# GpSimd steps that wait for the VectorE step ahead of them in a written plan

## The chip, the cores and the metric

The kernel runs on one core of a Trainium2 chip. Times are device microseconds of that core. The core has TensorE (PE: matrix products; PEld is its loading of weights), VectorE (DVE), ScalarE (ACT), GpSimd (POOL) and SyncE (SP), which here issues the transfers (DMA). Each engine works off its own instructions in order, and a semaphore makes one engine wait for another.

## What is computed

A chain of three layers on 3072 tokens with 256 channels (8 heads of 32). First an attention-like scan with decay, then two dense layers with nonlinearities (ELU, then Mish). Cut to what matters:

```python
def _attn_ref(x, a, B, C):                    # x 4x8x768x32, B and C 4x8x768x16
    log_a = np.log(np.clip(a, 1e-06, 1.0))
    state = np.zeros((batch, H, N, D))
    for c in range(S // 32):                  # chunks of 32 in the reference
        cum = np.cumsum(la, axis=-1)
        L = np.exp(cum[:, :, :, None] - cum[:, :, None, :]) * causal
        M = np.einsum('bhin,bhjn->bhij', Cc, Bc) * L
        y[:, :, sl] = (np.einsum('bhij,bhjd->bhid', M, xc)
                       + np.einsum('bhin,bhnd->bhid', Cc, state) * np.exp(cum)[..., None])
        Bx = np.einsum('bhjn,bhjd->bhjnd', Bc, xc) * np.exp(cum[:, :, -1:] - cum)[..., None, None]
        state = np.exp(np.sum(la, axis=-1))[..., None, None] * state + np.sum(Bx, axis=2)

h = x @ w_in;   g = np.where(h > 0, h, np.exp(np.minimum(h, 0)) - 1);          x = g @ w_out    # 256 -> 2048 -> 256
h = x @ w_in2;  g = h * np.tanh(np.log1p(np.exp(h)));                          y = g @ w_out2
```

## The kernel before

**Tiling.** The scan works on 32 tiles of 96 tokens of one batch (`T = 96`; 8 chunks by 4 batches). The dense layers work on seven blocks of tokens (`BL`: two of 384, four of 512, one of 256) in slots: 16 slots of 128 hidden channels for a layer and block. In a slot TensorE makes `h` (L780 to L782, written `emit_h`), the nonlinearity makes `w` from it, `w` is split into a high part `gh` (L366 or L368) and a low part `gl` (L823), and TensorE adds its product with the output weights to `acc` (L848 in the first block, L843 to L845 in layer 1, L874 and L875 in layer 2). The products that matter are made of three parts, high by high, low by high, high by low, so weights too are split: `raw` is put in order by L340 or L342, L351 and L358, its high part is taken by a cast (`job_4`: L366 on ScalarE, L368 on VectorE), its low part by a subtraction (`job_5`, L382 on GpSimd or VectorE). ELU is `elu_1` to `elu_3` (L796, L802 or L804, L810 or L812), Mish is L827. When a block of layer 1 is through, `acc` becomes the input of layer 2 by L855 (high, `xyh`) and L859 (low, `xyl`).

**The scan's steps.** For a tile a row of cumulated decays is loaded to all partitions (`d<-cum_d`), L553 subtracts (GpSimd or VectorE), L557 masks (GpSimd), L562 takes the exponential (ScalarE); `B` and `C` are split into three bf16 parts (L523, L528, L534, L540), transposed by DMA (L544), and TensorE makes scores (L670, or L658 in the first tiles), which L676 (L664) multiplies with the decays. GpSimd also makes `bw` (L567, L576) and the scaled `C` (L586), which L608 transposes on VectorE. L707 and L737 are the products of the tile with `x` and the new chunk state, L719 and L724 its split output.

**What sets the order.** No scheduler reorders this program. All work is written as steps: `step(opts, *deps, dl=...)` holds for each engine that could do it a cost, a function that emits its instructions, the steps it needs and a due time. `run_steps` plays the steps through once at build time, engine by engine, each time taking the most urgent one that can begin, and writes down for each step a begin time and the engine chosen. It keeps a list `lock` of the VectorE steps that can hold the SBUF port that VectorE and GpSimd share: the weight steps L342, L358, L368 and L382, the splits L528 and L540, L553, the copy behind L608, L804, and the splits `gh` and `gl`. In the plan a GpSimd step does not overlap one of these: `held[V]` and `held[G]` keep the end of the last on either side. At the end the steps are sorted by planned begin, and their functions are called in this order:

```python
        place = {k: i for i, (_, k, _) in enumerate(order)}
        for _, _, k, o in sorted((t, place[k], k, o) for t, k, o in order):
            steps[k][0][o][2]()
```

That fixes the order on each engine. Semaphore waits are put in by the layer below, for data and buffers alone. On the chip nothing holds GpSimd to the plan's order against VectorE: a GpSimd instruction starts when its data, its buffer and its own queue allow it.

Of the kernel before, what the change touches and what calls it, by code (L numbers as in the profile page):

```python
# [18 lines left out]
def tile_chain(  # L19
# [12 lines left out]
    nc = tc.nc  # L32
# [24 lines left out]
    at = ctx.enter_context(tc.tile_pool(name="at", bufs=1))  # L57
# [10 lines left out]
    steps = []  # L68
    A, V, G, PE, DQ = "act", "dve", "pool", "pe", "sp"
# [9 lines left out]
    lock = set()  # L79
# [3 lines left out]
    def step(opts, *deps, dl=1e9):  # L83
        steps.append((opts if isinstance(opts, list) else [opts], deps, dl))
        return len(steps) - 1
# [37 lines left out]
    def run_steps():  # L123
# [37 lines left out]
        while todo:  # L161
            k = todo.pop()
# [23 lines left out]
        def urgency(k, e):  # L186
            return late[k] + (HOLD if loads(k, e) else 0.0)
# [4 lines left out]
        def opened(k):  # L192
            for o, (e, cost, *_) in enumerate(steps[k][0]):
                open_[e].append((k, o, ready(k, e), cost))
# [11 lines left out]
        order = []  # L206
        for _ in range(n):
# [24 lines left out]
            t, e, can = best  # L232
            k, o, r, cost = min((c for c in can if c[2] <= t + 0.02), key=lambda c: (urgency(c[0], e), c[0]))
# [17 lines left out]
            for q in succ[k]:  # L251
                left[q] -= 1
                if not left[q]:
                    opened(q)
        place = {k: i for i, (_, k, _) in enumerate(order)}
        for _, _, k, o in sorted((t, place[k], k, o) for t, k, o in order):
            steps[k][0][o][2]()


    c_t, b_t, c96_t, x_t = {}, {}, {}, {}  # L260
# [496 lines left out]
    order = [(1, 0), (1, 1), (2, 0), (2, 1), (1, 2)]  # L757
# [37 lines left out]
    def elu_1(s):  # L795
        nc.scalar.activation(out=new_w(s), in_=st[s][0], func=AF.Exp)  # L796

    def elu_2(s, eng):
        w = st[s][1]
        st[s].append(eng)  # L800
        if eng == A:
            nc.scalar.activation(out=w, in_=w, func=AF.Relu, scale=-1.0, bias=1.0)  # L802
        else:
            nc.vector.tensor_scalar(out=w, in0=w, scalar1=1.0, scalar2=1.0, op0=ALU.min, op1=ALU.subtract)  # L804

    def elu_3(s):
        h, w, eng = st[s]
        st[s].pop()
        if eng == A:
            nc.vector.scalar_tensor_tensor(out=w, in0=w, scalar=-1.0, in1=h, op0=ALU.mult, op1=ALU.max)  # L810
        else:
            nc.vector.tensor_tensor(out=w, in0=h, in1=w, op=ALU.max)  # L812
# [13 lines left out]
    def mish_1(s):  # L826
        nc.scalar.activation(out=new_w(s), in_=st[s][0], func=AF.Mish)  # L827
# [49 lines left out]
    def y2_out1(c, k, eng):  # L877
        n = min(128, BL[c] - 128 * k)
        o = tl["o", c, k] = at.tile([128, DM], F32, tag="o", name="o", bufs=2)[0:n]
        if eng == V:  # L880
            nc.vector.tensor_scalar_mul(o, acc[2, c, k][:, 1], 1.0 / WS)
        else:
            nc.scalar.activation(out=o, in_=acc[2, c, k][:, 1], func=AF.Copy, scale=1.0 / WS)

    def y2_out2(c, k):
        o = tl["o", c, k]
        nc.vector.scalar_tensor_tensor(
            out=o, in0=acc[2, c, k][:, 0], scalar=1.0 / WS, in1=o, op0=ALU.mult, op1=ALU.add
        )
# [18 lines left out]
    def alt(f, *opts):  # L908

        return [(e, cost, lambda e=e: f(e)) for e, cost in opts]  # L910
# [256 lines left out]
    for s in range(len(order) * NF):  # L1167
# [23 lines left out]
        if layer == 1:  # L1191
            e = step((A, ca, lambda s=s: elu_1(s)), h, wn)
            table[e] = "exp"
            e = step(alt(lambda e, s=s: elu_2(s, e), (V, cv), (A, ca + 0.04)), e)
            lock.add(e)
            e = step((V, ct, lambda s=s: elu_3(s)), e)
        else:
            e = step((A, ca, lambda s=s: mish_1(s)), h, wn)
# [30 lines left out]
        else:  # L1229
            prev = YS.get(s - 1, [])  # L1230
            YS[s] = []
            for k in range(NK[c]):
# [4 lines left out]
                if f == NF - 1:  # L1237
                    of, on = take("o")
                    o = step(alt(lambda e, c=c, k=k: y2_out1(c, k, e), (A, 0.27), (V, 0.33)), y, on)
                    o = step((V, 0.35, lambda c=c, k=k: y2_out2(c, k)), o)  # L1240
                    q = step((DQ, 1.0, lambda c=c, k=k: y2_store(c, k), 0.36), o)
                    of.append(q)
                    acc_f[blk][k][0].append(o)
    run_steps()


# [28 lines left out]
```

## Time and profile before

| | |
|---|---|
| Runs | 622.65, 623.7, 625.8 us; median 623.7 |
| Profiled execution | 624.2 us, its span from the first to the last instruction 622.5 us |
| Busy, share of the span | PE 97%, PEld 82%, DVE 72%, ACT 61%, POOL 31% |
| Mean granted TensorE clock | 0.985 of 2.4 GHz |
| DMA | 47.09 MB, 46.29 MB of them on SyncE's queue |

The share of PE is an average over stages: in some it never pauses, in others it waits. How to read the rows further down: a row of the windows is a stretch of the execution with the busy time of each engine in it and its instructions in brackets; a row of the timeline is one instruction or a few alike, with start, duration, engine, line, what it writes from what, and in square brackets how long the engine was idle before it and what ended that.

### The profile page before, as it was taken

To read this page: it belongs to the slowest core of one execution; us is meant where nothing else is said; L and a number is where in the kernel's file an instruction comes from. 1 tells how busy PE (TensorE), PEld (TensorE's weight loads), DVE (VectorE), ACT (ScalarE), POOL (GpSimd) and SP (SyncE) were. 2 spreads that over 40 slices of the span, in tenths; PEclk is the share of its full clock that TensorE was granted. 3 is DMA by queue.
4 is the path that set the end of the run, shared out by engine and by line. 5 is a ranking of instruction groups with operands and counts; after the bars stand their busy time and mean duration, and the time that the engine had idled before them with its cause. 6 is when DMAs were issued, how large, how long until landed. Compare 5 with 4: busy or idle time off the path is not lost.

```text
span 622.5 us, 10990 instructions
## 1 busy us (share of the span) xinstructions
PE 602.3 (97%) x3876; PEld 508.4 (82%) x3876; DVE 450.5 (72%) x948; ACT 377.3 (61%) x705; POOL 191.6 (31%) x238
## 2 busy tenths in 40 slices
PE   6899989999999999999999999989999999999997
PEld 5777779989887878888887888877888888988896
DVE  4899988997798898765778865778865445744444
ACT  3699879976878865544687644588544214652121
POOL 2366455323554564201644501346200000200000
PEclk9599989999999999999999999999999999999999
DMA  7599893302647553001454301534200000100010
GB/s 159 162 261 292 261 246 86 60 12 55 128 85 89 112 98 85 11 0 28 84 110 75 87 1 14 107 63 99 56 4 1 0 1 4 34 1 0 1 35 17
DMA packets 133655, 47.09 MB, mean 76 GB/s; under 512 B 116672, under 2 KB 122432, under 8 KB 133600
## 3 DMA queue, kind: packets, MB, share of 16 engines
q1 hardware_dynamic: 133488, 46.29, 33.9%
q8 instruction: 30, 0.49, 0.3%
q14 instruction: 25, 0.20, 0.1%
q10 hardware_dynamic: 112, 0.10, 0.0%
HBM read 32.31 MB, written 3.24 MB: 57 GB/s over the span
## 4 chain that ended last, share of the span: by engine, by line
PE 77%; DVE 6%; ACT 6%; DMA 4%; issue 3%; SPq 2%; POOL 1%; DVEq 0%; POOLq 0%; ACTq 0%
PE acc L874 13%; PE h L780 12%; PE h L781 12%; PE h L782 12%; PE acc L875 6%; PE acc L843 6%; PE acc L844 6%; PE acc L845 6%; PE ys L707 2%; DMA t<-stk 1%; DMA bc<-in_B_dram 1%; PE s L670 1%; DMA xs<-in_x_dram 1%; DVE gl L823 1%; DVE raw L358 1%
## 5 line engine op out<-in xcount | busy, mean ns | idle before, releaser
L780 PE MATMUL h<-xyh,wi 128*128 128x512 f32 (+2 forms) x448 | 168.6, 376 | 2.0 <-ACT w L827 1.6
L781 PE MATMUL h<-xyl,wi 128*128 128x512 f32 (+2 forms) x448 | 162.0, 362 | 0.3 <-DVE xyl L724 0.3
L782 PE MATMUL h<-xyh,wi 128*128 128x512 f32 (+2 forms) x448 | 161.7, 361 | 0.0
L874 PE MATMUL acc<-wo,gh 128*128 128x512 f32 x384 | 142.6, 403 | 0.0
L823 DVE TENSOR_TENSOR gl<-w,gh 128x512 fp32r<-128x512 f32 (+2 forms) x181 | 119.2, 660 | 20.9 <-ACT gh L366 13.0
L827 ACT ACTIVATE w<-h 128x512 f32<-128x512 f32 (+2 forms) x112 | 59.4, 536 | 103.0 <-PE h L782 67.8
L875 PE MATMUL acc<-wo,gl 128*128 128x256 f32 x384 | 107.7, 280 | 0.2 <-DVE gl L823 0.2
L368 DVE CAST gh<-w 128x512 fp32r<-128x512 f32 (+2 forms) x114 | 47.8, 420 | 74.6 <-PE acc L874 50.3
L780 PEld LDWEIGHTS h<-xyh,wi 128*128 128x128 f32 x448 | 84.8, 189 | 19.0 <-ACT w L827 3.6
L782 PEld LDWEIGHTS h<-xyh,wi 128*128 128x128 f32 x448 | 84.9, 189 | 10.6
L781 PEld LDWEIGHTS h<-xyl,wi 128*128 128x128 f32 x448 | 85.0, 190 | 9.8 <-DVE xyl L724 0.7
L874 PEld LDWEIGHTS acc<-wo,gh 128*128 128x128 f32 x384 | 72.2, 188 | 15.4
L796 ACT ACTIVATE w<-h 128x512 f32<-128x512 f32 (+2 forms) x96 | 51.7, 539 | 54.6 <-PE h L782 34.7
L823 POOL TENSOR_TENSOR gl<-w,gh 128x512 fp32r<-128x512 f32 (+2 forms) x27 | 31.2, 1156 | 173.3 <-ACT gh L366 112.2
L875 PEld LDWEIGHTS acc<-wo,gl 128*128 128x128 f32 x384 | 72.6, 189 | 2.7 <-DVE gl L823 0.5
L843 PE MATMUL acc<-gh,wo 128*128 128x512 f32 (+2 forms) x192 | 71.0, 370 | 3.0 <-DVE xyl L859 3.0
L366 ACT ACTIVATE gh<-w 128x512 fp32r<-128x512 f32 (+2 forms) x94 | 54.8, 583 | 28.8 <-PE acc L844 22.5
L845 PE MATMUL acc<-gl,wo 128*128 128x512 f32 (+2 forms) x192 | 70.2, 366 | 0.0
L844 PE MATMUL acc<-gh,wo 128*128 128x512 f32 (+2 forms) x192 | 70.2, 365 | 0.0
L804 DVE TENSOR_SCALAR w<-w 128x512 f32<-128x512 f32 (+2 forms) x74 | 32.9, 444 | 26.0 <-ACT w L796 25.0
L812 DVE TENSOR_TENSOR w<-h,w 128x512 f32<-128x512 f32 (+2 forms) x74 | 46.6, 631 | 1.5
L843 PEld LDWEIGHTS acc<-gh,wo 128*128 128x128 f32 x192 | 36.7, 191 | 8.4 <-DVE xyl L859 3.4
(102 smaller groups left out, 847.8 us busy)
## 6 DMA issues: line engine op xcount, KB each, us to landing
d<-cum_d SPq DMA_DIRECT2D x31, 288.0 KB, 3.8
raw<-in_moe_w_in_dram SPq DMA_DIRECT2D x16, 512.0 KB, 6.7
raw<-in_moe_w_out_dram SPq DMA_DIRECT2D x16, 512.0 KB, 5.9
xs<-in_x_dram SPq DMA_DIRECT2D x32, 96.0 KB, 2.9
bc<-in_C_dram SPq DMA_DIRECT2D x32, 48.0 KB, 2.6
bc<-in_B_dram SPq DMA_DIRECT2D x32, 48.0 KB, 2.6
out_dram<-o SPq DMA_DIRECT2D x15, 96.0 KB, 1.9
bc<-bc SPq DMA_DIRECT2D x84, 16.0 KB, 2.4
```

The source lines that it names most:

```text
L366: nc.scalar.activation(out=out, in_=in_, func=AF.Copy)
L780: nc.tensor.matmul(out=h, lhsT=hi[:, k, fs], rhs=xh[:, k, :], start=(k == 0), stop=False)
L781: nc.tensor.matmul(out=h, lhsT=hi[:, k, fs], rhs=xl[:, k, :], start=False, stop=False)
L782: nc.tensor.matmul(out=h, lhsT=lo[:, k, fs], rhs=xh[:, k, :], start=False, stop=(k == 1))
L796: nc.scalar.activation(out=new_w(s), in_=st[s][0], func=AF.Exp)
L823: alu(eng).tensor_tensor(out=gl, in0=w, in1=gh.bitcast(F32), op=ALU.subtract)
L827: nc.scalar.activation(out=new_w(s), in_=st[s][0], func=AF.Mish)
L843: nc.tensor.matmul(out=y, lhsT=hi[:, f % FP, ds], rhs=gh, start=(f == 0), stop=False)
L844: nc.tensor.matmul(out=y, lhsT=lo[:, f % FP, ds], rhs=gh, start=False, stop=False)
L845: nc.tensor.matmul(out=y, lhsT=hi[:, f % FP, ds], rhs=gl, start=False, stop=(f == NF - 1))
L874: nc.tensor.matmul(out=y, lhsT=gh[:, ts], rhs=w[:, :, f % FP, :], start=(f == 0), stop=False)
L875: nc.tensor.matmul(out=y[:, 0], lhsT=gl[:, ts], rhs=w[:, 0, f % FP, :], start=False, stop=(f == NF - 1))
```

## The change

In the last loop of `run_steps`, the name of the last instruction of each VectorE step in `lock` is kept. The first instruction of the next GpSimd step in the plan's order gets a dependency on it, by semaphore, and the name is forgotten until the next such VectorE step. A second thing that the change's title speaks of, chunk states made for a pair of heads in a column group (`at_st`), stands in both kernels alike; the diff holds the waits alone.

```diff
@@ run_steps, at its end
         place = {k: i for i, (_, k, _) in enumerate(order)}
+        behind = mybir.DependencyInfo(mybir.DependencyClass.Sync, mybir.DependencyReason.DATA)
+        last = None
         for _, _, k, o in sorted((t, place[k], k, o) for t, k, o in order):
+            n0 = nc.n_instructions()
             steps[k][0][o][2]()
+            e = steps[k][0][o][0]
+            if e == V and k in lock:
+                last = list(nc.all_instructions())[-1].name
+            elif e == G and last is not None:
+                tc.add_manual_dep(list(nc.all_instructions())[n0], last, behind, reason="the order at the port")
+                last = None
```

No instruction changes its place on any engine; only what it waits for differs. The changed file has nine lines more above the steps, so its L391 is L382 of before, its L832 is L823, and so on.

GpSimd's queue before the gap at 85 us, from the second `gl` of layer 1's second block to the last weight split ahead of that gap, before:

```order
L823 TENSOR_TENSOR gl<-w,gh 128x384 [waits PE_49,Activation_49] x2
L586 TENSOR_TENSOR d<-bc,dk 32x384 [waits DMAHW5_49,DMAHW6_49,DMAHW4_49,Pool_49]
L382 TENSOR_TENSOR wo_1075<-raw_821,wo_1075 128x512 [waits DMAHW7_49,Activation_49,Pool_49]
L540 TENSOR_TENSOR stk<-r_1030,stk 96x8x16 [waits Activation_49]
L540 TENSOR_TENSOR stk<-r_1032,stk 96x8x16 [waits Activation_49]
L553 TENSOR_TENSOR d<-d,dk 96x384
L382 TENSOR_TENSOR wo_1111<-raw_840,wo_1111 128x512 [waits DMAHW0_49,Activation_49]
```

The same place of GpSimd's queue in the changed kernel (`DVE_49` is VectorE's semaphore):

```order
L832 TENSOR_TENSOR gl<-w,gh 128x384 [waits PE_49,Activation_49]
L832 TENSOR_TENSOR gl<-w,gh 128x384 [waits DVE_49,PE_49,Activation_49]
L595 TENSOR_TENSOR d<-bc,dk 32x384 [waits DMAHW5_49,DMAHW4_49,DMAHW6_49,DVE_49,Pool_49]
L391 TENSOR_TENSOR wo_1075<-raw_821,wo_1075 128x512 [waits DVE_49,DMAHW7_49,Activation_49,Pool_49]
L549 TENSOR_TENSOR stk<-r_1030,stk 96x8x16 [waits Activation_49]
L549 TENSOR_TENSOR stk<-r_1032,stk 96x8x16 [waits Activation_49]
L562 TENSOR_TENSOR d<-d,dk 96x384
L391 TENSOR_TENSOR wo_1111<-raw_840,wo_1111 128x512 [waits DMAHW0_49,DVE_49]
```

Nothing moved. The second `gl` now waits for VectorE's L382 at 79.72 us, the step L586 for VectorE's cast L368 at 82.70 us, the first L382 for VectorE's L382 at 86.06 us, the last one for VectorE's L823 at 91.09 us (by the numbers that the semaphores have to reach); the three between follow in the queue.

GpSimd's queue at 346 to 357 us, the splits and the mask of an attention tile, before:

```order
L823 TENSOR_TENSOR gl<-w,gh 128x512 [waits PE_49,DVE_49,Activation_49,Pool_49]
L586 TENSOR_TENSOR d<-bc,dk 32x384 [waits DMAHW5_49,DMAHW4_49,DMAHW6_49,DVE_49,Pool_49]
L540 TENSOR_TENSOR stk<-r_4455,stk 96x8x16 [waits DMAHW5_49,Activation_49]
L540 TENSOR_TENSOR stk<-r_4457,stk 96x8x16 [waits Activation_49]
L553 TENSOR_TENSOR d<-d,dk 96x384 [waits DMAHW6_49]
L557 AFFINE_SELECT d<-d 96x768 [waits DVE_49,Pool_49]
```

and in the changed kernel:

```order
L832 TENSOR_TENSOR gl<-w,gh 128x512 [waits PE_49,DVE_49,Activation_49,Pool_49]
L595 TENSOR_TENSOR d<-bc,dk 32x384 [waits DMAHW5_49,DMAHW4_49,DMAHW6_49,DVE_49,Pool_49]
L549 TENSOR_TENSOR stk<-r_4455,stk 96x8x16 [waits DMAHW5_49,DVE_49,Activation_49]
L549 TENSOR_TENSOR stk<-r_4457,stk 96x8x16 [waits Activation_49]
L562 TENSOR_TENSOR d<-d,dk 96x384 [waits DMAHW6_49]
L566 AFFINE_SELECT d<-d 96x768 [waits Pool_49]
```

The first split (L549, L540 of before) waits for VectorE's L823 at 355.19 us now, and with it what follows in the queue; where a row already waited for VectorE, the number it waits for has gone up, and the mask's own wait for VectorE is no longer needed.

## Rows read from the trace of the kernel before

**Rows 1.** Windows: stretch, length, busy of PE, PEld, DVE, ACT, POOL, PEclk, DMA, GB/s

```profile
20.00:50.00 30.00, 27.90 (x239) 21.48 (x232) 27.94 (x71) 25.01 (x51) 15.98 (x18) 0.83 0.88 230
50.00:75.00 25.00, 24.51 (x168) 18.06 (x167) 24.63 (x44) 23.42 (x47) 15.29 (x14) 1.00 0.90 273
75.00:90.00 15.00, 11.95 (x51) 9.65 (x50) 13.93 (x25) 11.14 (x25) 8.25 (x8) 0.94 1.04 261
90.00:110.00 20.00, 20.00 (x113) 20.00 (x112) 16.55 (x31) 18.81 (x40) 9.18 (x12) 0.96 0.40 107
110.00:135.00 25.00, 24.18 (x164) 22.45 (x164) 24.48 (x49) 22.97 (x40) 8.03 (x10) 1.00 0.24 43
...
335.00:400.00 65.00, 65.00 (x357) 53.55 (x356) 47.41 (x92) 32.89 (x61) 18.23 (x22) 1.00 0.23 46
400.00:440.00 40.00, 37.67 (x273) 30.59 (x272) 31.11 (x60) 32.19 (x54) 19.41 (x23) 1.00 0.38 81
```

**Rows 2.** Waits from 75 to 90 us: who for whom, us, times, longest

```profile
PE acc L843 <- DVE xyl L859: 3.0, 1, 3.0
```

**Rows 3.** Windows behind the gap, columns as in rows 1

```profile
88.36:91.40 3.04, 3.04 (x10) 3.04 (x10) 2.72 (x6) 1.97 (x4) 0.00 (x0) 0.50 1.03 171
91.40:94.40 3.00, 3.00 (x18) 3.00 (x18) 2.55 (x6) 2.62 (x6) 0.00 (x0) 0.98 0.97 204
```

**Rows 4.** Timeline of VectorE around the gap: start us, us, engine, line, operation

```profile
79.72 0.69 DVE L382 TENSOR_TENSOR wi<-raw,wi 128x512 fp32r<-128x512 f32 x1
...
80.78 1.04 DVE L358 SCALAR_TENSOR_TENSOR raw<-raw 128x512 int32<-128x512 int32 x1
81.98 0.80 DVE L804 TENSOR_SCALAR w<-w 128x384 f32<-128x384 f32 x1 [0.16 <-ACT w L796]
82.70 1.54 DVE L368 CAST wi<-raw 128x512 fp32r<-128x512 f32 x1
...
84.64 1.50 DVE L823 TENSOR_TENSOR gl<-w,gh 128x384 fp32r<-128x384 f32 x1
86.06 1.78 DVE L382 TENSOR_TENSOR wi<-raw,wi 128x512 fp32r<-128x512 f32 x1
87.76 1.01 DVE L859 SCALAR_TENSOR_TENSOR xyl<-acc,xyh 128x384 fp32r<-128x384 f32 x2
...
89.87 0.35 DVE L804 TENSOR_SCALAR w<-w 128x384 f32<-128x384 f32 x1
90.14 0.69 DVE L358 SCALAR_TENSOR_TENSOR raw<-raw 128x512 int32<-128x512 int32 x1
```

**Rows 5.** Timeline of GpSimd over the same stretch

```profile
79.89 1.37 POOL L823 TENSOR_TENSOR gl<-w,gh 128x384 fp32r<-128x384 f32 x1 [0.74 <-ACT gh L366]
81.34 1.22 POOL L586 TENSOR_TENSOR d<-bc,dk 32x384 f32<-32x384 f32 x1
82.64 1.32 POOL L382 TENSOR_TENSOR wo<-raw,wo 128x512 fp32r<-128x512 f32 x1
83.92 1.00 POOL L540 TENSOR_TENSOR stk<-r,stk 96x128 bf16<-96x128 f32 x2
...
85.68 1.60 POOL L382 TENSOR_TENSOR wo<-raw,wo 128x512 fp32r<-128x512 f32 x1
```

**Rows 6.** Timeline of ScalarE: the high part that L859 needs

```profile
83.93 0.84 ACT L855 ACTIVATE xyh<-acc 128x384 fp32r<-128x384 f32 x2
```

**Rows 7.** Groups of instructions by form: count, busy us, mean ns, idle before

```profile
L368 DVE CAST gh<-w 128x512 fp32r<-128x512 f32 x64 | 28.9, 451 | 56.2 <-PE acc L874 38.6 <-PE acc L844 12.3 <-ACT w L827 4.7
```

**Rows 8.** Timelines of GpSimd, VectorE and ScalarE around one mask

```profile
354.39 1.17 POOL L540 TENSOR_TENSOR stk<-r,stk 96x128 bf16<-96x128 f32 x2 [4.75 <-ACT stk L534]
...
356.87 0.88 POOL L557 TENSOR_SCALAR_AFFINE_SELECT d<-d 96x768 f32<-96x768 f32 x1
...
355.19 0.91 DVE L823 TENSOR_TENSOR gl<-w,gh 128x512 fp32r<-128x512 f32 x1
...
357.89 0.83 ACT L562 ACTIVATE d<-d 96x768 f32<-96x768 f32 x1
```

## The prediction

> **What bounds the kernel now.** I read the windows first: TensorE (PE) stands full or nearly so in most of the program, so only its gaps can be won. Between 20 and 75 us it is busy 27.90 of 30 and 24.51 of 25 us, from 75 to 90 us 11.95 of 15, from 90 to 110 us all 20 of 20, from 110 to 135 us 24.18 of 25, from 400 to 440 us 37.67 of 40 [rows 1]. The same rows show why the early part has gaps: VectorE (DVE) is busy 27.94 of 30, 24.63 of 25 and 13.93 of 15 us there, and ScalarE (ACT) 23.42 of 25 in the middle one. So from 20 to 90 us VectorE sets the pace with ScalarE close behind, and the largest gap is one of 3.0 us, in which PE's L843 waits for VectorE's L859 [rows 2]. After it PE runs at a granted clock of 0.50 for 3.04 us with 10 matmuls in it [rows 3], which is the 1.2 GHz level; the time at half speed belongs to that gap too.
>
> What VectorE does ahead of L859 is seen in its timeline against GpSimd's (POOL). L358 takes 1.04 us at 80.78 and 0.69 us at 90.14; L804 0.80 us at 81.98 and 0.35 us at 89.87; L382 1.78 us at 86.06 and 0.69 us at 79.72; L823 takes 1.50 us at 84.64 [rows 4]. Each long one starts while a GpSimd instruction is under way and ends about with it: L358 under L823 (79.89 + 1.37), L804 under L586 (81.34 + 1.22), the cast L368 of 1.54 us under L382 (82.64 + 1.32), L823 from the second L540 on (83.92 + 1.00 for the two), L382 under L382 (85.68 + 1.60) [rows 5]. So instructions of the two engines that work from SBUF run one after the other. It is no rare thing: against the shortest ones of each form I count 78 stretched VectorE instructions, from an L342 at 26.1 to an L823 at 436.9, some 40 us in all, 12 of them between 20 and 90 us.
>
> **The change, part by part.** No instruction moves on any engine and none that computes is added; there are waits alone. Read with their semaphore numbers, 95 of GpSimd's 238 instructions now wait for a later VectorE instruction than before. In the trace that one had ended already for 26 of them; 69 started ahead of that end, by 1.5 us in the median and 10 us at most. So GpSimd runs ahead of its plan today and will be held back to it.
>
> *The gap at 85 to 88 us.* I go through it by hand, with the waits of the changed order. GpSimd's second L823 waits for L382 (79.72 + 0.69 = 80.41) and starts 0.5 us later; VectorE's L358 behind it is held that much longer and ends at 82.3 in place of 81.82 [rows 4, 5]. GpSimd's L586 now stands behind the cast L368, its L382 behind VectorE's L382, and all that GpSimd does after that behind these, as its queue is in order. So L804 takes 0.35 us (to 82.65) and the cast some 0.45 us, the mean of the cast of that shape (to 83.1) [rows 4, 7]. Then L586 starts and takes its 1.22 us of today [rows 5], to 84.3; L812 reads PSUM and goes on beside it, L823 is held to 84.3 and ends 0.5 us behind that, as L358 does today behind GpSimd's L823 (81.82 and 81.26), so at 84.8; L382 takes 0.69 us to 85.5. L859 starts at 85.5 and not at 87.76, so 2.3 us earlier. The xyh that it needs is there: ScalarE's two L855 end at 84.77 [rows 6]. PE, which is done with its h at 85.3 (88.36 less the wait), waits some 0.7 us and not 3.0. **Term: -2.3 us**, bounds 0 (the L382 and L540 of GpSimd push in elsewhere) and -3.0 (the whole wait).
>
> *The clock behind it.* The 10 matmuls in 3.04 us are 0.30 apart [rows 3]; at full clock the same shape goes 18 in 3.00 us, 0.17 apart [rows 3]. With a gap of 0.7 us (those from 400 to 440 us, 2.3 us in all, leave the clock at 1.00 [rows 1]) I take it that the clock does not fall: **-1.3 us** (10 x 0.13), bounds 0 and -1.4.
>
> *20 to 75 us.* PE's gaps are 2.1 + 0.5 us [rows 1]. 8.4 us of the stretch lie there, 6.0 of them in instructions that GpSimd now has to follow; but ScalarE has only 1.6 us free from 50 to 75 us and PE itself is nearly full. **-0.5 us**, bounds 0 and -2.6.
>
> *The rest.* PE is idle 0.8 us from 110 to 135 us and 2.3 us from 400 to 440 us [rows 1]. In the first stretch VectorE is at 24.48 of 25 and GpSimd's steps, put behind those that they wait for, meet as many others as before (some 3 us each way): nothing. In the second a third of the collisions go: **-0.4 us**, bounds +1 and -2.3.
>
> *What the waits cost.* Behind a waiting GpSimd instruction stands its whole queue, and behind that SyncE's loads into tiles that GpSimd reads last. I moved each GpSimd instruction to the end of the one it now waits for and looked at those that wait for it. Of TensorE's none is late (the nearest keeps 0.4 us). SyncE's loads come up to 10 us later, after 85 us some weight loads by 5 us, but what comes over 2 us late is first read 11 us or more after it lands today. Ten instructions of ScalarE and VectorE are late, by 8 us together. One such: VectorE's L823 at 355.19 lasts 0.69 us when undisturbed, so L540 starts at 355.95 and not at 354.39, and the mask L557 behind it, for which ScalarE's L562 waits (end 357.75, start 357.89), comes 1.6 us later [rows 8]. From 335 to 400 us PE is never idle [rows 1], with several slots of work ahead of it; so **+0.4 us**, bounds 0 and +6 (below).
>
> Sum: -2.3 - 1.3 - 0.5 - 0.4 + 0.4 = **-4.1 us**. The profiled execution took 624.2 us (its span is 622.5), which gives 620.1; the median of the runs is 623.7, 0.5 less, so I forecast **619.6 us**.
>
> The Trainium skill (SBUF — State Buffer, "Who interferes with whom") says that the shared pair is held for the whole instruction by whoever issues first, and that issue order decides who blocks. That speaks against this change: GpSimd's turn is not spared, only put behind another. The trace agrees on the lock, with L382 of 1.78 us against 0.69. It is the mechanism of the first rival, which stands on rows by itself.
>
> **Rivals.** *The collisions only move.* GpSimd's instructions still need as long, and a VectorE instruction that follows does not wait for them in the program, it runs into them. Against it: in the walk above, L859 and L812, which read PSUM, take the places in which GpSimd goes on. For it: from 110 to 135 us I find no gain, and if GpSimd's L586 and the L382 behind it met L823 and L382 in turn (1.22 + 1.32 us), L859 would start at 86.8, PE would wait 1.5 us, the clock might fall all the same, and the saving would be given back where VectorE is full again. Time: 623.7 - 1 to + 1, so **623.5 us**.
>
> *All gaps near collisions close.* Then 20 to 75 us gives its 2.6 and 400 to 440 us some 1.5 as well: 619.6 - 2.1 - 1.1, **616.4 us**.
>
> *Slower: the mask chain.* ScalarE's in-order queue is held at L562 (or L534) by a GpSimd step that is now behind VectorE; the slack is 0.14 us, the delay 1.6 us, so 1.5 us a time [rows 8]. It decides where the attention tile is what PE waits for, as from 400 to 440 us; with four such tiles it is 6 us and eats the gain: 619.6 + 6, and with the gap at 85 us kept besides (2.3) **628 us**. Against it: PE is full from 335 to 400 us, right where the slack is 0.14.
>
> That the waits do nothing (all met in time, or implied) is out: 69 are unmet in the trace.
>
> **How the numbers follow.** Forecast 0.46 (617 to 621.5), collisions only move 0.30 (622 to 625), all gaps 0.11, slower 0.13. About 0.5%, 3.1 us, is what a measurement of this kernel can tell from no change: faster means under 620.6. Of the forecast's 0.46, 0.39 lie below that; with 0.11 that is 0.50 faster. Same: 0.07 + 0.29 = 0.36. Slower: 0.13 + 0.01 = 0.14. The range goes from 615.5, below the all-gaps case, to 625.5, above that of the moved collisions, and leaves out most of the slower case.
>
> **What would show it.** In the changed profile: L859 at about 85 us and no wait of PE above 1 us there; no stretch at clock 0.50 around 90 us; VectorE's L358 and L382 means down, with GpSimd's idle time put down to VectorE; GpSimd's steps 1 to 5 us later between 60 and 150 us. Wrong if PE still waits 2 to 3 us for L859, or if ScalarE's waits for GpSimd at L562 and L534 grow while PE's gaps from 165 to 440 us exceed today's.

## The result, and the profile after

| | before | after |
|---|---|---|
| Median of the runs taken side by side | 624.38 us (622.65 to 625.8) | 614.27 us (613.71 to 615.25) |
| Span of the profiled execution | 622.5 us | 612.1 us |

The ratio is 0.9841, with a 95% interval of 0.9811 to 0.9871. The forecast was 619.6 us in a range of 615.5 to 625.5: the direction and the main place were right, the gain was 10.1 us and not 4.1, and the time lies 1.2 us below the range.

The page of the changed kernel gives busy time, share of the span and number of instructions of each engine:

```profile
PE 598.7 (98%) x3876; PEld 506.4 (83%) x3876; DVE 433.2 (71%) x948; ACT 377.4 (62%) x705; POOL 177.6 (29%) x238
```

Before, VectorE was busy 450.5 us and GpSimd 191.6 us, with the same instructions. Waiting inside an instruction counts as busy there, so 17.3 and 14.0 us of it are gone. Against the short ones of each form, 52 of VectorE's instructions are stretched by over 60 ns, 21.7 us in all; before 78, 39.7 us (with the very shortest as the measure it is 55 and 22.8 us, before 78 and 41.1). All of them, in both traces, are of the lines in `lock`, and each starts while a GpSimd instruction is under way. The page's chain that ended last, by engine, is now almost TensorE alone (before: PE 77%, DVE 6%, ACT 6%, DMA 4%):

```profile
PE 92%; DMA 3%; ACT 2%; DVE 1%; issue 1%; SPq 0%; ACTq 0%; DVEq 0%
```

The windows of after, in the stretches and columns of [rows 1]:

```profile
20.00:50.00 30.00, 28.20 (x232) 22.07 (x225) 27.55 (x73) 25.40 (x51) 14.15 (x19) 0.81 0.89 234
50.00:75.00 25.00, 25.00 (x171) 18.27 (x170) 22.17 (x52) 24.56 (x50) 13.53 (x14) 1.00 0.90 274
75.00:90.00 15.00, 15.00 (x78) 13.46 (x77) 13.28 (x24) 14.89 (x32) 8.11 (x9) 1.00 1.08 265
90.00:110.00 20.00, 20.00 (x118) 20.00 (x117) 18.68 (x35) 19.28 (x39) 10.09 (x13) 1.00 0.44 107
110.00:135.00 25.00, 24.79 (x170) 22.94 (x169) 22.83 (x49) 21.23 (x37) 6.88 (x8) 1.00 0.16 33
335.00:400.00 65.00, 64.77 (x382) 53.14 (x381) 45.95 (x95) 35.97 (x63) 18.34 (x24) 1.00 0.28 53
400.00:440.00 40.00, 39.80 (x260) 32.76 (x259) 28.59 (x59) 30.87 (x55) 17.57 (x22) 1.00 0.41 79
```

PE no longer pauses from 50 to 110 us, the granted clock stays at 1.00 there, and from 400 to 440 us PE pauses 0.2 us where it paused 2.3 (0.4 with the pause of 0.2 us at 399 us, as the same work stands 10 us earlier in after). VectorE has 2.8 us to spare from 50 to 75 us, where it had 0.4.

Both traces have the same 3876 matmuls, but for some ten places in the same order, so I compare when the same one starts, after minus before. This says where the time went:

| up to (us of before) | after minus before | step |
|---|---|---|
| 57 | -0.9 us | -0.9, at 8 to 9.4 us |
| 74 | -1.9 | -1.0 |
| 92, behind the gap and the half clock | -6.6 | -4.75 |
| 134 | -7.6 | -1.0 |
| 190 | -8.1 | -0.5 |
| 400 | -8.2 | -0.1 |
| 410 | -9.9 | -1.6 |
| 426 and to the end | -10.35 | -0.5 |

The first step is no part of the change: it is there as well in two experiments whose waits begin only at 92 and 380 us of the plan, and missing in one that has all the early ones. At its place the same matmuls (L483 of before) start 0.11 us apart in after and 0.21 us apart in before. Nor is the step from 134 to 190 us shown to be the change's: e10_late, which has no new wait there, shows -0.4 us as well. That leaves some 9.0 us for the waits, the half clock among them.

**The gap at 85 us.** VectorE's timeline in after, at the place of [rows 4]:

```profile
76.22 0.68 DVE L391 TENSOR_TENSOR wi<-raw,wi 128x512 fp32r<-128x512 f32 x1
...
77.29 1.35 DVE L367 SCALAR_TENSOR_TENSOR raw<-raw 128x512 int32<-128x512 int32 x1
78.56 0.35 DVE L813 TENSOR_SCALAR w<-w 128x384 f32<-128x384 f32 x1
78.83 0.41 DVE L377 CAST wi<-raw 128x512 fp32r<-128x512 f32 x1
...
80.41 0.56 DVE L832 TENSOR_TENSOR gl<-w,gh 128x384 fp32r<-128x384 f32 x1 [0.70 <-PE acc L857]
80.89 0.69 DVE L391 TENSOR_TENSOR wi<-raw,wi 128x512 fp32r<-128x512 f32 x1
81.49 1.02 DVE L868 SCALAR_TENSOR_TENSOR xyl<-acc,xyh 128x384 fp32r<-128x384 f32 x2
```

GpSimd's timeline in after, at the place of [rows 5]; the brackets are the new waits:

```profile
77.07 1.02 POOL L832 TENSOR_TENSOR gl<-w,gh 128x384 fp32r<-128x384 f32 x1 [1.20 <-DVE wi L391]
79.38 0.86 POOL L595 TENSOR_TENSOR d<-bc,dk 32x384 f32<-32x384 f32 x1 [1.29 <-DVE wi L377]
81.80 1.32 POOL L391 TENSOR_TENSOR wo<-raw,wo 128x512 fp32r<-128x512 f32 x1 [1.56 <-DVE wi L391]
83.08 0.81 POOL L549 TENSOR_TENSOR stk<-r,stk 96x128 bf16<-96x128 f32 x2
```

One collision is left of the five of before: L367 (L358 of before) runs into GpSimd's L832 and takes 1.35 us. The small L813, the cast, the `gl` and the second L391 have their short times, since GpSimd starts when they are through and works while VectorE waits for PE or does L868, which reads PSUM. TensorE's timeline of after at the first matmul that waits for L868 shows no pause:

```profile
83.11 0.33 PE L791 MATMUL h<-xyh,wi 128*128 128x384 f32 x1
83.29 0.33 PE L852 MATMUL acc<-gh,wo 128*128 128x384 f32 x1
```

L852 is the L843 of [rows 2], which waited 3.0 us. The half clock of [rows 3] is gone with it.

### The profile page after: what moved, and what is told of

Same layout as the page of the kernel before. It is cut to its first block, busy times and chain, and to the rows that moved or that the text cites. A ratio compares the mean times of both kernels' runs of the same rounds, so it can differ in the third digit from the quotient of the medians.

```text
span 612.1 us, 10993 instructions
## 1 busy us (share of the span) xinstructions
PE 598.7 (98%) x3876; PEld 506.4 (83%) x3876; DVE 433.2 (71%) x948; ACT 377.4 (62%) x705; POOL 177.6 (29%) x238
## 4 chain that ended last, share of the span: by engine, by line
PE 92%; DMA 3%; ACT 2%; DVE 1%; issue 1%; SPq 0%; ACTq 0%; DVEq 0%
PE h L789 15%; PE h L790 14%; PE h L791 14%; PE acc L883 14%; PE acc L884 7%; PE acc L852 6%; PE acc L853 6%; PE acc L854 6%; PE acc L857 4%; PE ys L716 2%; DMA t<-stk 2%; PE s L667 2%; PE s L679 1%; ACT L836 1%; PE ys L746 1%
## 5 line engine op out<-in xcount | busy, mean ns | idle before, releaser
L832 DVE TENSOR_TENSOR gl<-w,gh 128x512 fp32r<-128x512 f32 (+2 forms) x181 | 122.5, 678 | 21.5 <-ACT gh L375 12.9
L832 POOL TENSOR_TENSOR gl<-w,gh 128x512 fp32r<-128x512 f32 (+2 forms) x27 | 29.6, 1096 | 147.6 <-ACT gh L375 95.6
L852 PE MATMUL acc<-gh,wo 128*128 128x512 f32 (+2 forms) x192 | 70.2, 365 | 0.0
L853 PE MATMUL acc<-gh,wo 128*128 128x512 f32 (+2 forms) x192 | 69.6, 362 | 0.0
L813 DVE TENSOR_SCALAR w<-w 128x512 f32<-128x512 f32 (+2 forms) x74 | 30.5, 414 | 26.2 <-ACT w L805 25.2
L595 POOL TENSOR_TENSOR d<-bc,dk 32x384 f32<-32x384 f32 x28 | 27.9, 999 | 68.8 <-DVE gl L832 41.8
```

Of the source, the lines that this page charges most:

```text
L832: alu(eng).tensor_tensor(out=gl, in0=w, in1=gh.bitcast(F32), op=ALU.subtract)
L852: nc.tensor.matmul(out=y, lhsT=hi[:, f % FP, ds], rhs=gh, start=(f == 0), stop=False)
L853: nc.tensor.matmul(out=y, lhsT=lo[:, f % FP, ds], rhs=gh, start=False, stop=False)
```

## The experiments

All are edits in the loop at the end of `run_steps`. What is shown of them is cut to the lines that count and stands against the changed kernel, for e7_mirror against the kernel before. The theory: the order at the shared port is what counts, each GpSimd step behind the VectorE step that the plan puts ahead of it, in a few places where somebody waits for VectorE. The rival: any wait that holds GpSimd back would do, since it thins its work out where VectorE is full.

**Which places.** Five kernels keep the waits of one stretch of planned time (`t` is the planned begin):

```diff
-        for _, _, k, o in sorted((t, place[k], k, o) for t, k, o in order):
+        for t, _, k, o in sorted((t, place[k], k, o) for t, k, o in order):
...
-                tc.add_manual_dep(list(nc.all_instructions())[n0], last, behind, reason="the order at the port")
+                if t < 92:
+                    tc.add_manual_dep(list(nc.all_instructions())[n0], last, behind, reason="the order at the port")
```

The condition is `t < 92` in e1_front (18 waits), `t >= 92` in e2_back (77), `62 <= t < 92` in e9_gap (9), `92 <= t < 200` in e11_mid (27), `t >= 380` in e10_late (21).

> Only the GpSimd steps that are planned before 92 us wait (18 of the 95 waits). Comparing the two profiles by TensorE's matmuls, number by number, the changed kernel is 0.9 us ahead at 57 us, 1.9 at 74, 6.6 at 92 (the gap behind L859 and the half clock after it), 7.6 at 140, 8.2 at 200 to 400, 10.3 from 420 on. Theory (collisions at the port, counted where VectorE sets the pace): this kernel keeps what is won up to 92 us and loses the rest, 624.4 - 6.6 = 617.8 us, 617 to 619. Rival (what is won early is lost again if the later order is the old one, or the later gains hang on the early ones): 614 or 622.

> Only the GpSimd steps planned from 92 us on wait (77 waits). Theory: the early gap of 3 us and the half clock behind it come back, and 3.7 us are won later (1.0 from 110 to 135 us, 0.5 from 165 to 190, 2.1 from 400 to 425): 620.7 us, 619.5 to 622. Rival (later gains need the earlier start): 624. The two halves should add to the whole, 10.1 us.

> Only the GpSimd steps planned from 62 to 92 us wait (9 waits that VectorE did not have to meet before, from an L382 on weights at 62 us to an L823 at 95 us). Theory: the whole gap behind L859 goes with these nine, with the half clock after it: 4.75 us and the 1 us ahead of it, 624.4 - 5.5 = 619 us, 618 to 620. Rival (the gap closes only because VectorE is early from 24 us on): 622 us or more.

> Only the GpSimd steps planned from 92 to 200 us wait (27 waits). Theory: 0.8 us are won at 126 to 134 us and 0.5 at 165 to 190, as in the changed kernel: 623 us, 622 to 623.7. Rival (these gains need the early start): 624.4.

> Only the GpSimd steps planned from 380 us on wait (21 waits). Theory: TensorE's two waits at 406 to 409 us and the one at 421 to 425 us go by 2.1 us in all through the VectorE steps next to them: 622.3 us, 621.5 to 623. Rival (they go because loads and steps stand otherwise from 92 us on): 624.4.

| kernel | median us | ratio to before (95%) | steps in its trace against before (us of before) |
|---|---|---|---|
| e1_front | 618.47 | 0.9894 (0.9861 to 0.9927) | -4.75 at 92 us; constant to 0.6 us behind it |
| e9_gap | 620.03 | 0.9937 (0.9911 to 0.9963) | -4.75 at 92 us |
| e2_back | 619.5 | 0.9922 (0.9887 to 0.9956) | -1.4 at 88 to 92 (the clock, below), -1.0 by 134, -0.4 by 190, -0.7 at 327 (not in after), -1.7 at 409, -0.9 at 425 us |
| e11_mid | 623.05 | 0.9972 (0.9946 to 0.9997) | +2.6 at 42 (granted clock 0.50 from 42.2 to 45.6), -1.0 at 70, -2.4 at 88 to 92, -1.0 by 134, -0.4 by 190 us |
| e10_late | 622.54 | 0.9968 (0.9944 to 0.9992) | -1.4 at 88 to 92 (the clock), -0.4 by 190, -1.7 at 409, -0.6 at 425 us |

Nine waits ahead of the gap bring its whole step, though the median of e9_gap just misses what was expected. e1_front and e2_back share the waits between them, and their gains, 6.6 and 4.9 us by the ratios, sum to 11.5, the whole to 10.1; with some 2 us of uncertainty on each they add. But for the clock's, and for that of 190 us in e10_late, the steps stand where the waits are, and what is won early is not given back: between the steps of e1_front and e9_gap the difference moves by 0.6 us at most.

e2_back also tells the clock's part from the gap's. TensorE's timeline in it still has the gap:

```profile
87.70 0.45 PE L853 MATMUL acc<-gh,wo 128*128 128x384 f32 x1 [3.09 <-DVE xyl L869]
```

but the window behind it in e2_back, columns as in [rows 1], is at full clock:

```profile
87.70:90.70 3.00, 3.00 (x17) 3.00 (x18) 2.69 (x6) 1.92 (x4) 0.00 (x0) 1.00 0.83 156
```

So it has 17 matmuls where [rows 3] has 10. Against before's profiled execution it is 0.7 us ahead in front of the pause and 2.05 us at 92 us: 1.4 us for the clock alone.

**Order or mere holding back.** e3_one_earlier lets a GpSimd step wait for the port-holding VectorE step that precedes the one of after; e6_six_earlier goes five back (8 waits are unmet then); e5_scalar takes ScalarE's preceding step.

```diff
...
 # e3_one_earlier
-                last = list(nc.all_instructions())[-1].name
-            elif e == G and last is not None:
-                tc.add_manual_dep(list(nc.all_instructions())[n0], last, behind, reason="the order at the port")
-                last = None
+                fresh, older, last = True, last, list(nc.all_instructions())[-1].name
+            elif e == G and fresh:
+                if older is not None:
+                    tc.add_manual_dep(list(nc.all_instructions())[n0], older, behind, reason="one step earlier")
+                fresh = False
 # e6_six_earlier: the same with the sixth name from the end, line[-6]
 # e5_scalar
-            if e == V and k in lock:
+            if e == A:
```

> Each waiting GpSimd step waits for the locking VectorE step before the one that it waits for in the changed kernel: 49 waits unmet in the trace of before against 71, by 1.7 us in the median against 1.8, so GpSimd is held back nearly as much, but the last VectorE step is free to be met. Theory (it is the order against that one step): stretched VectorE time goes back up to 30 us or more from 22, the gap at 85 us is there at least in part, 619 to 623 us. Rival (GpSimd held back at all, which shifts its reads and SyncE's loads, is what helps): 613 to 616 us.

> Each GpSimd step waits for the ScalarE step that precedes it in the plan, none for VectorE beyond its data. That holds GpSimd back to about its planned time, but leaves open which of it and VectorE comes first. Theory now (any wait that keeps GpSimd from running ahead of VectorE's queue does it, because VectorE's next step is off before GpSimd has the word; without VectorE's own word the collisions stay): stretch of VectorE 28 us or more, 617 to 622 us. Rival (GpSimd late is enough, whoever holds it): stretch near 20 us, 613 to 616 us.

> Each waiting GpSimd step waits for the locking VectorE step five before the one of the changed kernel; only 8 of these waits are unmet in the trace of before (71 in the changed kernel, 49 with one step earlier). Theory: the gain goes with the waits that are unmet, so GpSimd runs ahead again: stretch 33 us or more, 621 to 625 us. Rival (what counts is a few places where GpSimd is far ahead): 616 us or less.

| kernel | median us | ratio to before (95%) | VectorE stretched by |
|---|---|---|---|
| after | 614.27 | 0.9841 (0.9811 to 0.9871) | 21.7 us |
| e3_one_earlier | 614.25 | 0.9828 (0.9796 to 0.986) | 19.6 us |
| e5_scalar | 621.66 | 0.9953 (0.9937 to 0.997) | 33.6 us |
| e6_six_earlier | 623.76 | 0.9982 (0.9965 to 0.9999) | 37.8 us |

e5 and e6 came out as the theory has it. e5 holds GpSimd back too and closes the early gap (-5.8 us at 91 us), but its waits know nothing of the port and it is later than before elsewhere (+1.8 us at 238 us, +1.0 at 310, +1.1 at 437), so of the 10 us 3 are left. e6 keeps the gap, 2.2 us and half clock, and has the half clock once more behind 409 us (the last section has it). e3 missed its expectation: it is as fast as after. The reason is seen at the same place. VectorE's timeline of e3:

```profile
81.31 0.69 DVE L392 TENSOR_TENSOR wi<-raw,wi 128x512 fp32r<-128x512 f32 x1
```

and GpSimd's timeline of e3, with the step that the plan puts behind this one:

```profile
81.53 1.66 POOL L392 TENSOR_TENSOR wo<-raw,wo 128x512 fp32r<-128x512 f32 x1 [1.20 <-issue]
```

GpSimd's instruction begins 0.22 us behind VectorE's, which keeps its 0.69 us; GpSimd's takes 1.66 us where it takes 1.32 in after, and ends at the same place, 83.1 to 83.2. When the step before last ends, VectorE's next one is off before GpSimd's can be. So one step earlier still means the plan's order at the port here; elsewhere the stretch of 19.6 us says as much, and e3 does not speak for the rival.

**The order the other way, and both ways.** In e7_mirror only VectorE's port-holding step waits, for the GpSimd step that precedes it; in e4_both each side waits for the other.

```diff
 # e7_mirror
...
+            if e == G:
+                turn = list(nc.all_instructions())[-1].name
+            elif e == V and k in lock and turn is not None:
+                tc.add_manual_dep(list(nc.all_instructions())[n0], turn, behind, reason="the order at the port")
+                turn = None
 # e4_both: this and the waits of after
```

> The other half of the plan alone: each locking VectorE step waits for the GpSimd step before it in the plan, GpSimd waits for nothing new. Theory: GpSimd is ahead of the plan today, so these waits are mostly met, the collisions with GpSimd's early steps stay: stretch 30 us or more, 622 to 627 us. Rival (either order at the port will do): 614 to 618 us.

> As the changed kernel, and each locking VectorE step waits for the GpSimd step before it in the plan as well. Theory (GpSimd first is what hurts, VectorE first costs little): the stretch of VectorE turns into waits for GpSimd, which are as long or longer, since now a late GpSimd step holds VectorE even when the port is free: 613 to 618 us, no gain. Rival (what is left, 22 us of stretch, is lost for want of order the other way): 611 us or less.

e7_mirror took 627.91 us, 1.0065 (1.0041 to 1.0089): slower than before, a little above what was expected, with 33.2 us of stretch. e4_both took 620.19 us, 0.9922 (0.9897 to 0.9947), slower than expected, and slower than after by 6 us although no VectorE instruction is stretched at all (0.0 us). What the port no longer costs, the semaphores seem to. VectorE's waits for GpSimd in e4_both (who for whom, us, times, longest), of which the list of after has none:

```profile
DVE gl L837 <- POOL d L571: 6.4, 7, 1.4
DVE gl L837 <- POOL d L567: 5.4, 6, 1.5
...
DVE gh L382 <- POOL d L600: 3.4, 4, 1.0
...
DVE gh L382 <- POOL d L571: 3.1, 4, 1.1
```

So the splits `gh` and `gl`, which feed PE, now wait for GpSimd's masks (L571), its subtractions (L567) and its scaled `C` (L600). Two windows of e4_both, columns as in [rows 1]:

```profile
110.00:135.00 25.00, 23.46 (x160) 21.38 (x160) 23.08 (x53) 22.17 (x38) 5.70 (x7) 1.00 0.15 34
...
400.00:440.00 40.00, 38.54 (x263) 31.35 (x260) 25.49 (x61) 31.77 (x57) 17.73 (x24) 1.00 0.33 66
```

PE pauses 1.5 us in each, in after 0.2 us. That these pauses come from the splits' waits I read from their size and place; I have not followed each.

**Behind any VectorE step.** e8_any_vector waits for the last VectorE step of any kind, also those outside `lock`, none of which is stretched in any of these traces (157 waits).

```diff
-            if e == V and k in lock:
+            if e == V:
```

> Each GpSimd step waits for the VectorE step of any kind before it in the plan, those that read PSUM and cannot be met included: 157 waits, 145 of them unmet in the trace of before. Theory: the stretch is that of the changed kernel, 18 to 22 us, and the longer hold begins to cost where ScalarE waits for masks and splits: 613.5 to 618 us. Rival (the more GpSimd is held, the better): 612 us or less.

632.69 us, 1.013 (1.0101 to 1.0159), and the stretch is 42.7 us, more than before, where I had expected 18 to 22. A GpSimd step that starts behind a VectorE step which holds nothing starts just as the next one wants the port, and then VectorE is the late one. VectorE's timeline of e8 at one such place:

```profile
237.85 1.01 DVE L685 TENSOR_TENSOR r<-s,d 96x384 f32<-96x384 f32 x2
238.78 1.21 DVE L832 TENSOR_TENSOR gl<-w,gh 128x512 fp32r<-128x512 f32 x1
```

and GpSimd's:

```profile
238.48 0.97 POOL L595 TENSOR_TENSOR d<-bc,dk 32x384 f32<-32x384 f32 x1 [3.62 <-DVE r L685]
```

Of e8's 104 stretched instructions (44.0 us against the very shortest), 32 with 15.0 us start under a GpSimd instruction whose wait ended with a VectorE step outside `lock`; in after it is one, with 0.6 us. GpSimd is late as well; ScalarE's waits for it in e8:

```profile
ACT d L571 <- POOL d L566: 18.4, 16, 3.9
...
ACT w L805 <- POOL gl L832: 14.2, 8, 3.9
```

The same in after:

```profile
ACT d L571 <- POOL d L566: 7.4, 6, 2.5
ACT w L805 <- POOL gl L832: 7.3, 8, 1.4
```

Before, the two were 5.8 and 5.5 us. So the waits of the slower rival's chain exist, and in e8 they are about three times as long; that they are what makes e8 slow I have not followed as far as PE. The change itself adds only 3.4 us to them, and no pause of PE in after is longer than the like one before.

## Why the prediction was right or wrong

| term | predicted | by the steps of the traces |
|---|---|---|
| gap at 85 to 88 us and the clock behind it | -2.3 and -1.3 | -4.75 together |
| 20 to 75 us | -0.5 | -1.0 |
| 110 to 135 us | 0 | -1.0 (from 92 us on) |
| 135 to 190 us | not in the sum | -0.5, not shown to be the change's |
| 8 to 9.4 us | not in the sum | -0.9, not the change's |
| 400 to 440 us | -0.4 | -2.1 |
| what the waits cost | +0.4 | nothing seen on PE |

The mechanism was right and the sum too small. The steps that failed are two terms. That of 400 to 440 us was sized as a share of the collisions (-0.4, measured -2.1), and that of the gap with its clock let VectorE set out too late (-3.6, measured -4.75). Besides, 110 to 135 us was put at nothing and gave about 1.0, 20 to 75 us gave twice its 0.5, and the cost of the waits did not show. The 0.9 us at 8 to 9.4 us are chance.

**Right.** The reading that VectorE's long instructions ahead of L859 are GpSimd's turns at the port, that the gap [rows 2] is made of them, and that no consumer on PE comes late. The Trainium skill (SBUF — State Buffer, "Who interferes with whom") says that who issues first holds the shared pair for a whole instruction and the other blocks; e3's 0.69 beside 1.66 us agrees. I had held this rule against the change, as a turn that is only put behind another. The traces show why it isn't: of VectorE's stretched time 18 us disappear, because a GpSimd step that starts right behind a port-holding one lies beside VectorE's waits and its work from PSUM. GpSimd is busy beside the lines in `lock` for 98 us before and 60 after, beside VectorE's other instructions for 65 and 80, beside an idle VectorE for 28 and 38.

**The gap term was too small: the walk began too late.** From the end of L382 at 80.41 us [rows 4] to the start of L859 I forecast 5.1 us; it took 4.6 (76.90 to 81.49), against 7.35 before. That part was nearly right. But I let VectorE arrive at that L382 when it does today. It arrived 3.5 us earlier (76.22 for 79.72), as its stretch from 50 to 75 us had fallen from 5.9 to 1.2 us (e9_gap, with no new wait before 62 us, arrives at 76.24); PE came to the place only 1.9 us earlier (its last matmul of `h` starts at 83.11 for 84.97). So the lead is worth 1.6 us and the shorter walk 0.5; the wait of 0.7 us that I left is gone, and VectorE has over 1 us in hand. The 20 to 75 us term was sized by PE's gaps inside the stretch; what VectorE gains there and PE can't use is not lost, it is lead at the next gap.

**The rest was too small: collisions were counted as alike.** For 400 to 440 us I took a third of the collisions off and so a fraction of PE's pauses, -0.4. The trace of before shows what PE's pauses there hang on. VectorE's timeline of before:

```profile
396.18 1.25 DVE L823 TENSOR_TENSOR gl<-w,gh 128x512 fp32r<-128x512 f32 x1
397.46 0.88 DVE L368 COPY r<-r 32x384 f32<-32x384 f32 x1
398.38 1.05 DVE L540 TENSOR_TENSOR stk<-r,stk 96x128 bf16<-96x128 f32 x2
...
404.84 0.55 DVE L553 TENSOR_TENSOR d<-d,dk 96x384 f32<-96x384 f32 x1 [2.22 <-DMA d<-cum_d]
```

GpSimd's of before at that place, under which the first three are stretched:

```profile
396.05 2.07 POOL L553 TENSOR_TENSOR d<-d,dk 96x384 f32<-96x384 f32 x2
398.20 0.88 POOL L557 TENSOR_SCALAR_AFFINE_SELECT d<-d 96x768 f32<-96x768 f32 x1
```

SyncE's queue of before, where the transpose needs L540 and the load of the next decays stands behind the transpose:

```profile
399.49 1.46 SPq L544 DMA_TRANSPOSE t<-stk  x1
401.04 1.03 SPq L516 DMA_DIRECT2D d<-cum_d  x1
```

And TensorE's pauses of before at the end of it:

```profile
407.29 0.38 PE L670 MATMUL s<-t 96*96 96x96 bf16 x4 [0.84 <-DVE xyl L724]
...
409.26 0.51 PE L780 MATMUL h<-xyh,wi 128*128 128x512 f32 x1 [0.83 <-ACT w L827]
```

The late L553 also holds back VectorE's L747. ScalarE's L719 starts 0.1 us behind the end of that one in both traces (at 406.45 us, and at 396.58 in after), and L827, for which the second pause waits, stands behind L719 in ScalarE's queue.

In after the same VectorE instructions are short, and two splits further down are long in their place; VectorE's timeline of after:

```profile
387.95 0.69 DVE L832 TENSOR_TENSOR gl<-w,gh 128x512 fp32r<-128x512 f32 x1
388.67 0.36 DVE L377 COPY r<-r 32x384 f32<-32x384 f32 x1
389.06 0.49 DVE L549 TENSOR_TENSOR stk<-r,stk 96x128 bf16<-96x128 f32 x2
...
391.04 1.36 DVE L832 TENSOR_TENSOR gl<-w,gh 128x512 fp32r<-128x512 f32 x1
...
392.86 1.17 DVE L832 TENSOR_TENSOR gl<-w,gh 128x512 fp32r<-128x512 f32 x1
...
394.97 0.56 DVE L562 TENSOR_TENSOR d<-d,dk 96x384 f32<-96x384 f32 x1 [0.94 <-DMA d<-cum_d]
```

GpSimd's L562 of after now waits for that L549:

```profile
389.62 1.03 POOL L562 TENSOR_TENSOR d<-d,dk 96x384 f32<-96x384 f32 x1 [1.77 <-DVE stk L549]
```

From the first `gl` to the load's issue (L516, L525 of after) it took 4.86 us and takes 3.22 (SyncE's row of after follows); TensorE's first pause is gone and the second is 0.23 us (its row stands last):

```profile
391.17 1.06 SPq L525 DMA_DIRECT2D d<-cum_d  x1
```

```profile
399.39 0.50 PE L789 MATMUL h<-xyh,wi 128*128 128x512 f32 x1 [0.23 <-ACT w L836]
```

So a share of the collisions says nothing here: those ahead of the transpose went, and those that came are where no pause of PE follows. e10_late, with 21 late waits, shows the same two steps (-1.7 and -0.6 us). I should have followed each of PE's pauses [rows 1] back and asked whether a stretched instruction is on its chain. For 110 to 135 us I set the collisions lost against those newly met, some 3 us each way; VectorE's stretch there fell from 2.8 to 0.9 us.

**The clock's term came true with luck.** I took from the short pauses between 400 and 440 us [rows 1] that a pause of 0.7 us leaves the clock at 1.00. In after no pause is left to try it on, and e6_six_earlier and e11_mid fell to 0.50 behind pauses of 0.8 us and less, while e2_back and e10_late did not behind 3.1 us. So the 1.4 us are won against an execution like before's profiled one and, as it seems, not against each.

**The waits cost nothing that shows on PE.** L562's wait for the mask [rows 8] grew as feared on ScalarE (5.8 to 7.4 us in the whole run), but no pause of PE grew.

**The rivals.** That collisions only move (0.30) is out: e1_front and e9_gap keep the whole early gain, and the stretch is nearly halved. All gaps near collisions (616.4 us, 0.11) was the right picture and still 2 us short, for it left out 92 to 190 us and PE's lead. The range ended 1.2 us too high for the same reason: I took the all-gaps case as the best that could be, though the lower bounds of the terms, with PE's 0.8 us from 110 to 135 us [rows 1], sum to -3.0 - 1.4 - 2.6 - 0.8 - 2.3 = -10.1 us, which is the gain that was measured.

What stays open: the stretches e11_mid and e10_late give 1.75 and 2.0 us by their ratios with intervals of 1.6 us each way, so the smaller steps are known from the traces, one execution of each kernel, rather than from the times.

## What to carry to other kernels

Where VectorE and GpSimd both work from SBUF, compare each form's long instructions with its short ones and look at whether a GpSimd instruction lies under them; then ask of each pause of the bounding engine whether one of these is on its chain, for only those are worth an order. Let the engine that isn't urgent wait for the urgent one's port-holding step, by a semaphore on it: the reverse, or both ways, or a wait for just any step, cost 6 to 18 us against it here. Sum gains along the program and not place by place, since what one stage gains and can't use is lead at the next gap.

## What was unexpected of the hardware

- After a pause of TensorE of 3.0 us the granted clock was 0.50 for some 3 us in before's profiled execution [rows 3], and so it was after 3.3 us in e7_mirror and 2.2 us in e6_six_earlier, but it stayed at 1.00 behind the pauses of 3.1 us in e2_back and e10_late. That is worth 1.4 us. It fell behind shorter pauses too: in e11_mid at 42.2 us behind 0.5 and 0.6 us (2.6 us lost), in e6_six_earlier behind 0.8 us twice, which in before left it at 1.00. The window of e6_six_earlier behind the second of these:

```profile
409.67:413.09 3.42, 3.42 (x11) 2.75 (x10) 0.89 (x2) 3.37 (x6) 1.18 (x2) 0.50 0.34 46
```

- In e3_one_earlier the VectorE instruction that is first at the port is not slowed at all by a GpSimd instruction that begins 0.22 us behind it (0.69 us, the short time), and with the semaphore one step back the kernel is as fast as with one on the step itself (614.25 and 614.27 us).
- No stretched instruction at all (e4_both) is not the fastest: 21.7 us of stretch in the right places beat 0.0 us by 6 us.
